# Two moves in VectorE's written order: batch 3's column maxima between the two halves of the fourth operand sum, batch 0's second softmax finished behind batch 2's own

## The chip, the cores and the metric

One NeuronCore of a Trainium2 chip runs the whole kernel. The metric is the device time of one execution in microseconds. Engine names below are those of the profile: PE is TensorE's matmuls and PEld its weight loads, DVE is VectorE, ACT is ScalarE, POOL is GpSimd, SP is the engine whose queue issues most of the DMAs.

## The reference

Cross-attention in both directions between 512 tokens and 32 state rows, for 8 batches of 8 heads, and behind it a feed-forward block on all rows.

```python
B, H, S, Ns, D = (8, 8, 512, 32, 64)
n_tokens, d_model, d_ff = (4608, 512, 2048)
...
scores = scale * np.matmul(x, state.transpose(0, 1, 3, 2))
scores = scores - scores.max(-1, keepdims=True)
a = np.exp(scores)
a /= a.sum(-1, keepdims=True) + 1e-09
xread = np.matmul(a, state)
scores2 = scale * np.matmul(state, x.transpose(0, 1, 3, 2))
scores2 = scores2 - scores2.max(-1, keepdims=True)
a2 = np.exp(scores2)
a2 /= a2.sum(-1, keepdims=True) + 1e-09
sread = np.matmul(a2, x)
return np.concatenate([xread, sread], axis=2).astype(np.float32)
...
h = x @ w_in
g = np.maximum(0.01 * h, h)
return (g @ w_out).astype(np.float32)
```

The second line of code gives the default sizes of the block; here it works on B x (512 + 32) = 4352 rows. The first softmax (of a token over the 32 state rows) feeds `xread`, the second (of a state row over the 512 tokens) feeds `sread`.

## The kernel before

**Tiling.** A batch's scores are one PSUM tile `sc` of 128 x 1024: the partitions hold 32 state rows for each of four heads, two such groups lie side by side, and the columns are the tokens. There is one `sc` bank pair for all batches, which also takes one of the products `pm` further on. The kernel does not form `xread`: it multiplies the state with `w_in` first (`a_m`, result `pm`, copied into SBUF as `M` by `m_evict` or by the copies at L1221 and L1229), and `ff1` multiplies `M` with the transposed probabilities `aT`. Each `ff1` makes 128 of the 2048 hidden rows for the batch's 512 tokens in a PSUM tile `ph`, two matmuls of 512 columns, and ACT's leaky ReLU (L398) writes it to `hT`. There are two `ph` buffers.

**The product with `w_out`** is done with seven half-size products instead of eight (`Fast` and `Batch`). They run in the order 1, 2, 6, 5, 7, 3, 4, and each has 8 units `(n, m)` of two matmuls (L674). Their left operands are parts of `hT` or sums of parts: four sums numbered 0 to 3, tiles `su0` to `su3`, computed on DVE by `sums` at L663. Each can be done in halves, `sums(n, 0, 4)` for units 0 to 3 and `sums(n, 4, 8)` for units 4 to 7. Product 6 takes sum 1, product 5 takes sum 0, product 7 takes sum 2, product 3 takes sum 3. Sum 1 is an input of sum 3. Product 4 takes a weight sum, the tile `tw_x` written at L640. Products 1, 6, 5 and 7 are saved by ACT (L683), the results are joined by DVE (L686) and by POOL (L746), and go out by DMA.

**First softmax of a batch.** `a_shift` finds each token's block maxima in `sc` (L221), spreads them (L229) and subtracts them (L234, result `sh`); `a_exp` is ACT's exponential (L241); `a_probs` sums, inverts and multiplies (L246 to L259, result `aT`).

**Second softmax.** `a_max2` takes the maxima along the rows of `sc`, one DVE reduce of 128 x 1024 (L283) and a small scaling of its 128 x 2 result (L285, `mcols`). `a_exp2` is two exponentials on ACT, one for each half of `sc` (L291); they need `mcols`, and they are the last readers of `sc`. `a_probs2` is what remains of that softmax: DVE adds 1e-9 to the 128 x 2 row sums (L297) and inverts them into the tile `qall` (L299). Nothing else is done there for batches 0 to 6: `a_sread_rows` multiplies the unnormalized `sread` (PSUM tile `psn`) with `qall` while it copies it out (L346).

**The order.** It is written out by hand: each engine runs its instructions in the order in which the program emits them, and waits only for semaphores. The loop over `b` runs batches 2 to 7, 16 steps `s` each. A step emits one `ff1` of batch `b` and some units of batch `b - 1`'s product with `w_out`. For `b == 2` the numbers of units are `PACE2 = (1, 2, 0, 4, 4, 4, 4, 4, 4, 4, 4, 4, 4, 5, 5, 5)`. Twelve of batch 1's 56 units are emitted ahead of the loop and four in steps 0 to 2, so steps 3 and 4 hold product 6, steps 5 and 6 product 5, steps 7 and 8 product 7, steps 9 and 10 product 3, and steps 11 and 12 product 4. Behind step 11's units PE runs the three `a_m` of batch 3, whose second writes into the `sc` banks and whose third takes both `ph` buffers.

DVE's part is emitted much earlier than PE needs it. In step 3 of `b == 2` the program emits, for DVE and in this order: `a_probs2(a0)`, the scaled copy in `a_sread_rows([a0])`, the first part of batch 3's `a_shift`, all of sum 2 of batch 1, the second part of `a_shift`, `a_max2` of batch 3, and the two halves of sum 3 of batch 1. Behind them, from step 7, come the second half of `tw_x` (L640), batch 3's `a_probs` and, from step 10, the join of product 3.

Four POOL copies `cast_x` of batch 4's tokens (L111) and POOL's copy of the later state rows (L181) are emitted in steps 3 and 4. SP's queue transposes batch 4's tokens by DMA behind that (L195, tile `xT`), for batch 4's scores in the next `b`.

Ahead of the loop, batch 2's `a_exp` and `a_probs` are emitted behind `piece(0, h0, 1, 3, copy=VEC)`, and what DVE gets next is the copy of batch 2's second `M` chunk (`m_evict(a2, 1, pm[0], VEC)`, L385).

Of the kernel before, what the change touches and what calls it, by code (L numbers as in the profile page):

```python
# [30 lines left out]
def kernel(  # L31
# [75 lines left out]
    def open_xb(b):  # L107
        xs[b] = xpool.tile([P, NT, H, D], BF16, name="xb", tag="xb")
# [80 lines left out]
    def a_open(a, b):  # L189
        a.b = b  # L190
        a.xb = xs[b]
        a.xT = att.tile([P, NT, NK, P], BF16, name="xT", tag="xT")
# [26 lines left out]
    def block_max(flat, n):  # L219
        m1 = att.tile([P, n], FP32, name="mrow", tag="mrow")  # L220
        nc.vector.tensor_reduce(  # L221
            out=m1[:], in_=flat.rearrange("p (c j) -> p c j", j=NS),
            axis=AX.X, op=ALU.max, apply_transpose=True,
        )
        return m1

    def block_rows(m1, n):
        m1b = att.tile([P, n, NS], FP32, name="mrowb", tag="mrowb", bufs=1)
        nc.vector.transpose(m1b[:], m1[:, :, None].to_broadcast([P, n, NS]))  # L229
        return m1b  # L230

    def block_sub(flat, m1b, n):
        sh = att.tile([P, n * NS], FP32, name="sh", tag="sh", bufs=1)
        nc.vector.tensor_tensor(  # L234
            out=sh[:], in0=flat, in1=m1b[:].rearrange("p c j -> p (c j)"), op=ALU.subtract,
        )
        return sh
# [26 lines left out]
    def a_shift(a, part=None):  # L264
        flat = a.sc[:].rearrange("p g c -> p (g c)")
        if part != 1:
            a.mb = block_rows(block_max(flat, NB), NB)
        if part != 0:
            a.sh = block_sub(flat, a.mb, NB)

    def a_exp(a):
        a.e1 = block_exp(a.sh, NB)

    def a_probs(a, part=None):
        if part != 1:
            a.q1h = block_recip(a.e1, NB)
        if part != 0:
            a.aT = att.tile([P, 2, S], BF16, name="aT", tag="aT")
            block_probs(a.aT[:], a.e1, a.q1h, NB)

    def a_max2(a):
        m2 = att.tile([P, 2], FP32, name="mcol", tag="mcol")
        nc.vector.tensor_reduce(out=m2[:], in_=a.sc[:], axis=AX.X, op=ALU.max, negate=True)  # L283
        a.m2s = att.tile([P, 2], FP32, name="mcols", tag="mcols")
        nc.vector.tensor_scalar(out=a.m2s[:], in0=m2[:], scalar1=SCALE, scalar2=None, op0=ALU.mult)  # L285
# [10 lines left out]
    def a_probs2(a):  # L296
        nc.vector.tensor_scalar(out=a.r2[:], in0=a.r2[:], scalar1=1e-9, scalar2=None, op0=ALU.add)  # L297
        q2 = qall[:, a.b]
        nc.vector.reciprocal(q2, a.r2[:])  # L299
        if a.b == B - 1:  # L300
            a.a2 = att.tile([P, 2, S], BF16, name="a2", tag="e2", bufs=3)
            for g in range(2):
                nc.vector.tensor_scalar(
                    out=a.a2[:, g, :], in0=a.e2[:, g, :],
                    scalar1=q2[:, g:g + 1], scalar2=None, op0=ALU.mult,
                )
# [456 lines left out]
    a0, a1, a2 = att_of[:3]  # L763
# [283 lines left out]
    before = Batch(1, h1)  # L1047
# [34 lines left out]
    piece(0, h0, 1, 3, copy=VEC)  # L1082
    a_exp(a2)
    a_probs(a2)
    a_open(att_of[3], 3)
    a_xt_dma(att_of[3])
    ff(10, 12, 13)
# [21 lines left out]
    for b in range(2, B):  # L1109
        hT = hpool.tile([P, 16, S], BF16, name="hT", tag="hT")  # L1110
        a = att_of[b]
        nxt = att_of[b + 1] if b + 1 < B else None
        now = Batch(b, hT)

        def fill(s):
            units((PACE2 if b == 2 else PACE)[s])

        def units(n):
            left = min(n, len(before.units))
            if left:  # L1120
                before.run(left)
            if n > left:
                now.run(n - left)

        ms = 11 if b == 2 else 10
        for s in range(16):
            fast = nxt is None and 4 <= s < 12
            if fast:
                n = 1 if s in (7, 11) else 2
                k = PACE[s]  # L1130
                for i in range(n):
                    fl.product()
                    units((i + 1) * k // n - i * k // n)
            elif s == ms + 1:
                fill(s)
            elif s == 0 and b == 2:
                units(1)
            if not fast:
                ff1(a, hT, 4 + s if nxt is None and s < 4 else s)
            if s == 0:  # L1140
                if b + 2 < B:
                    load_x(b + 2, nc.sync)
                a_a2t(a)
                for n in (0, 1):
                    before.f.sums(n, 4, 8)
            elif s == (3 if b == 2 else 1):
                if nxt is not None:
                    a_scores(nxt)
                m_evict(a, 3, a_m(a, 3, "big"), SCA)
                if b == 2:  # L1150
                    a_probs2(a0)
                    a_sread_rows([a0])
                elif b % 2:
                    a_sread_rows([att_of[b - 2], att_of[b - 1]])
                if b == 2:
                    a_shift(nxt, 0)
                    before.f.sums(2)
                    a_shift(nxt, 1)
                    a_max2(nxt)
                    before.f.sums(3, 0, 4)  # L1160
                    before.f.sums(3, 4, 8)
                elif nxt is not None:
                    a_shift(nxt)
                if b + 2 < B:
                    open_xb(b + 2)
                    for h in range(0, H, 2):
                        cast_x(b + 2, h, h + 2, POO)
                if b > 2:
                    before.f.sums(2, 4, 8)
            elif s == 3:  # L1170
                before.f.sums(3)
                if nxt is not None:
                    a_max2(nxt)
            elif s == 4:
                if b == 2:
                    state_t(1)
                elif b == 4:
                    sread_t(0, 3)
                elif b == 7:
                    sread_t(1, 4)  # L1180
            elif s == 8:
                if nxt is None:
                    a_sread(a)
            elif s == (13 if b == 2 else 12):
                for n in range(3):
                    now.f.sums(n, 0, 4)
            if nxt is None:
                if s == 1:
                    fl = FastLast(a, hT)
                    fl.sums()  # L1190
                elif s in (6, 10):
                    fi.w_sum({6: 1, 10: 3}[s])
                elif s == 13:
                    fl.flush()
                    fi.x_sums()
            elif b >= B - 3 and s == 14:
                if b == B - 3:
                    fi = FastIn(None)
                fi.w_sum(2 * (b - (B - 3)))
            if s == (9 if b == 2 else 7) and b + 2 < B:  # L1200
                a_open(att_of[b + 2], b + 2)
                a_xt_dma(att_of[b + 2])
            if nxt is not None:
                if b == 2 and s < ms:
                    if s in (8, 9):
                        a_exp2(nxt, s - 8)
                    elif s == 7:
                        a_exp(nxt)
                        weights_sum(3, 0, 4)
                        a_probs(nxt, 0)  # L1210
                elif s == 5:
                    a_exp(nxt)
                elif s in (7, 8):
                    a_exp2(nxt, s - 7)
                    if s == 7:
                        a_probs(nxt)
                elif s == ms + 1:
                    for some in ((a1, a2, nxt) if b == 2 else (nxt,)):
                        a_probs2(some)
                elif s in (ms + 2, ms + 3):  # L1220
                    SCA(nxt.M[:, s - ms - 2, DM:2 * DM], pm1[:, s - ms - 2, :])  # L1221
            if s != ms + 1 and not fast:
                fill(s)
            if s == ms and nxt is not None:
                pm0 = a_m(nxt, 0, "big")
                pm1 = a_m(nxt, 1, "sc")
                pm2 = a_m(nxt, 2, "ph")
                for g, copy in enumerate((VEC, SCA)):
                    copy(nxt.M[:, g, 2 * DM:3 * DM], pm2[g][:])  # L1229
                m_evict(nxt, 0, pm0, SCA)  # L1230
                if b == 2:
                    a_probs(nxt, 1)
        before = now
# [90 lines left out]
```

## Time and profile before

| | us |
|---|---|
| median of 3 runs | 203.46 (203.34 to 203.77) |
| the profiled execution's own time | 203.29 |
| its span, first to last instruction | 201.5 |
| PE busy | 194.9 (97%) |
| DVE busy | 160.4 (80%) |
| ACT busy | 144.1 (72%) |
| POOL busy | 54.3 (27%) |

All times in the rows further down are microseconds from the span's start. A row of the timeline gives start, duration, engine, line, operation, the tiles written and read with their shapes, the count of instructions merged into it, and in brackets how long the engine was idle before it and what ended that. Neighbouring matmuls overlap in their durations, so their distance is read from start to start. In the view of waits, the numbers are the total, the count and the longest.

### The profile page before, as it was taken

The numbers are of one execution on the slowest core, as the hardware profiler recorded it, in microseconds if no ns is written. First come the engines' busy times: TensorE is split into PE (matmuls) and PEld (weight loads), VectorE is DVE, ScalarE is ACT, GpSimd is POOL, SyncE is SP. The second block draws the span as 40 slices with busy tenths as digits, with TensorE's granted clock in tenths as the row PEclk, the third lists the DMA queues.
The fourth block names the chain that finished last, engine by engine and source line by source line (L and its number), as shares of the span: only waits on it lengthen the run. The fifth ranks groups of instructions, "written<-read, shape, count | busy, mean of one in ns | idle before, by whom it ended". The sixth has DMA issues, their size and how long they took to land.

```text
span 201.5 us, 4991 instructions
## 1 busy us (share of the span) xinstructions
PE 194.9 (97%) x2066; PEld 134.4 (67%) x2066; DVE 160.4 (80%) x246; ACT 144.1 (72%) x264; POOL 54.3 (27%) x79
## 2 busy tenths in 40 slices
PE   7799999999999999999999999999999999999992
PEld 2467644346676667766776677676767688799881
DVE  1666779998999989975997599779978977995622
ACT  3468837699877866978697868787878768767610
POOL 8751065591028004200420040200020024004250
PEclk9999999999999999999999999999999999999998
DMA  6999997999581894449433844290025102310035
GB/s 166 226 208 258 249 293 132 217 278 219 109 228 28 236 281 74 93 176 265 84 71 143 279 72 87 104 157 6 0 107 156 29 0 89 123 55 0 0 96 167
DMA packets 40470, 28.01 MB, mean 139 GB/s; under 512 B 25280, under 2 KB 37696, under 8 KB 40448
## 3 DMA queue, kind: packets, MB, share of 16 engines
q1 hardware_dynamic: 35248, 20.88, 41.3%
q0 software_dynamic: 4912, 6.55, 15.8%
q10 hardware_dynamic: 288, 0.26, 0.5%
q8 instruction: 16, 0.26, 0.5%
q14 instruction: 6, 0.05, 0.1%
HBM read 17.30 MB, written 8.91 MB: 130 GB/s over the span
## 4 chain that ended last, share of the span: by engine, by line
PE 74%; DMA 14%; DVE 6%; ACT 2%; POOL 1%; issue 1%; POOLq 0%; DVEq 0%
PE yq L674 40%; PE ph L392 19%; DMA xl<-in_x_dram 10%; DMA w_in_bf<-in_moe_w_in_dram 4%; PE pf L470 3%; PE yu L674 3%; PE pm L371 3%; DVE su L663 2%; PE pl L559 2%; PE psn L337 1%; PE py L603 1%; PE phw L405 1%; PE sc L211 1%; ACT e L291 1%; DVE mrowb L229 1%
## 5 line engine op out<-in xcount | busy, mean ns | idle before, releaser
L398 ACT ACTIVATE hT<-ph 128x512 bf16<-128x512 f32 x100 | 58.7, 604 | 18.5 <-PE ph L392 18.1
L392 PE MATMUL ph<-aT,M 128*128 128x512 bf16 x200 | 57.9, 379 | 0.0
L674 PEld LDWEIGHTS <-su 128*128 128x128 bf16 x480 | 45.8, 98 | 15.4 <-DVE su L663 1.9
L674 PEld LDWEIGHTS <-hT 128*128 128x128 bf16 x336 | 32.3, 98 | 14.3 <-issue 2.5
L674 PE MATMUL yq<-tw_xf,su 128*128 128x256 bf16 x224 | 31.6, 273 | 0.0
L674 PE MATMUL yq<-w_out_bf,hT 128*128 128x256 bf16 x224 | 31.0, 273 | 0.0
L111 POOL CAST xb<-xl 128x512 bf16<-128x512 f32 (+1 forms) x24 | 13.4, 604 | 48.8 <-DMA xl<-in_x_dram 37.6
L663 DVE TENSOR_TENSOR su<-hT 128x1024 bf16<-128x1024 bf16 (+1 forms) x27 | 19.3, 718 | 6.7 <-ACT hT L398 6.7
L392 PEld LDWEIGHTS <-M 128*128 128x128 bf16 x200 | 19.4, 98 | 5.7 <-issue 0.5
L746 POOL TENSOR_TENSOR yo<-sv,sv 128x512 f32<-128x512 f32 x7 | 9.5, 1358 | 41.2 <-issue 20.8
L683 ACT COPY sv<-yq 128x512 f32<-128x512 f32 x28 | 16.3, 586 | 3.0 <-PE yq L674 2.2
L674 PE MATMUL yq<-w_out_bf,su 128*128 128x256 bf16 x112 | 15.3, 273 | 0.4 <-DVE su L663 0.4
L674 PE MATMUL yq<-tw_x,su 128*128 128x256 bf16 x112 | 15.5, 273 | 0.0
L686 DVE TENSOR_TENSOR yo<-yq,sv 128x512 f32<-128x512 f32 x20 | 13.6, 682 | 1.5 <-PE yq L674 1.5
L674 PE MATMUL yq<-tw_x,hT 128*128 128x256 bf16 x104 | 14.5, 273 | 0.0
L385 ACT CAST M<-pm 128x1024 bf16<-128x1024 f32 x12 | 12.2, 1019 | 0.2 <-PE pm L371 0.2
L291 ACT ACTIVATE e<-sc,mcols 128x512 bf16<-128x512 f32 x16 | 11.0, 696 | 0.1
L603 PEld LDWEIGHTS <-hT 128*128 128x128 bf16 x64 | 5.9, 98 | 7.2 <-issue 1.1
L663 DVE TENSOR_TENSOR su<-su,hT 128x1024 bf16<-128x1024 bf16 x14 | 9.7, 692 | 0.5
L283 DVE TENSOR_REDUCE mcol<-sc 128x2 f32<-128x1024 f32 x8 | 9.7, 1216 | 0.0
L221 DVE TRANSPOSE_TENSOR_REDUCE mrow<-sc 128x32 f32<-128x1024 f32 x7 | 8.7, 1242 | 0.5 <-PE sc L211 0.5
L663 DVE TENSOR_TENSOR su<-hT,su 128x2048 bf16<-128x2048 bf16 (+1 forms) x8 | 9.0, 1134 | 0.0
(173 smaller groups left out, 301.7 us busy)
## 6 DMA issues: line engine op xcount, KB each, us to landing
out_dram<-yo SPq DMA_DIRECT2D x12, 512.0 KB, 2.7
xl<-in_x_dram SPq DMA_DIRECT2D x5, 1024.0 KB, 6.8
w_in_bf<-in_moe_w_in_dram POOLq DMA_DIRECT2D x4, 512.0 KB, 9.6
w_out_bf<-in_moe_w_out_dram POOLq DMA_DIRECT2D x4, 512.0 KB, 17.4
xf<-in_x_dram SPq DMA_DIRECT2D x2, 512.0 KB, 5.5
x<-in_x_dram POOLq DMA_DIRECT2D x2, 512.0 KB, 13.9
xl<-in_x_dram POOLq DMA_DIRECT2D x1, 1024.0 KB, 20.1
out_dram<-ysb SPq DMA_DIRECT2D x4, 256.0 KB, 5.6
```

The lines of the kernel that those rows point to most:

```text
L111: copy(xs[b][:, :, h0:h1].rearrange("p t h d -> p h t d"), xl[b][:, h0:h1].rearrange("p h (t d) -> p h t d", t=NT),)
L221: nc.vector.tensor_reduce(out=m1[:], in_=flat.rearrange("p (c j) -> p c j", j=NS), axis=AX.X, op=ALU.max, apply_transpose=True,)
L283: nc.vector.tensor_reduce(out=m2[:], in_=a.sc[:], axis=AX.X, op=ALU.max, negate=True)
L291: nc.scalar.activation(out=a.e2[:, g], in_=a.sc[:, g, :], func=AF.Exp, bias=a.m2s[:, g:g + 1], scale=SCALE, accum_out=a.r2[:, g:g + 1],)
L385: copy(a.M[:, :, cols], pm[:])
L392: nc.tensor.matmul(ph[:], lhsT=a.M[:, g, P * j:P * (j + 1)], rhs=a.aT[:, g, :], start=(g == 0), stop=(g == 1),)
L398: nc.scalar.activation(out=hT[:, j, :], in_=ph[:], func=AF.Prelu, alpha=0.01)
L663: (eng or nc.vector).tensor_tensor(out=S[n][:, ms], in0=u[:, ms], in1=v[:, ms], op=op)
L674: nc.tensor.matmul(bank[:, i, :], lhsT=lhs[:, m, P * i:P * (i + 1)], rhs=rhs[:, m, :], start=(first and m == 0 and (i == 0 or of is not No ...
L683: copy(t[:], bank)
L686: nc.vector.tensor_tensor(out=dst, in0=bank, in1=self.sv[n][:], op=ALU.add)
L746: nc.gpsimd.tensor_tensor(out=self.yo(1)[:, :, HC:], in0=f.sv[7][:], in1=f.sv[5][:], op=ALU.add)
```

## The change

Two edits, both in DVE's order alone. No instruction is added or removed, and no other engine's order changes.

1. `a_probs2(a0)` (L297 and L299, batch 0) leaves its place ahead of `a_sread_rows([a0])` in step 3 of `b == 2` and goes ahead of the loop, right behind batch 2's `a_probs`.
2. In the same step, `sums(3, 0, 4)` of batch 1 is emitted ahead of `a_max2` of batch 3 instead of behind it. `sums(3, 4, 8)` stays behind.

```diff
@@ -1082,6 +1082,7 @@
     piece(0, h0, 1, 3, copy=VEC)
     a_exp(a2)
     a_probs(a2)
+    a_probs2(a0)
     a_open(att_of[3], 3)
     a_xt_dma(att_of[3])
     ff(10, 12, 13)
@@ -1148,7 +1149,6 @@
                     a_scores(nxt)
                 m_evict(a, 3, a_m(a, 3, "big"), SCA)
                 if b == 2:
-                    a_probs2(a0)
                     a_sread_rows([a0])
                 elif b % 2:
                     a_sread_rows([att_of[b - 2], att_of[b - 1]])
@@ -1156,8 +1156,8 @@
                     a_shift(nxt, 0)
                     before.f.sums(2)
                     a_shift(nxt, 1)
+                    before.f.sums(3, 0, 4)
                     a_max2(nxt)
-                    before.f.sums(3, 0, 4)
                     before.f.sums(3, 4, 8)
                 elif nxt is not None:
                     a_shift(nxt)
```

## The prediction

> **What bounds the kernel now.** I read the page's busy shares first, then PE's waits behind the place of the change, then the timelines of PE and DVE there.
>
> ```profile
> PE 194.9 (97%) x2066; PEld 134.4 (67%) x2066; DVE 160.4 (80%) x246; ACT 144.1 (72%) x264; POOL 54.3 (27%) x79
> ```
>
> ```profile
> PE yq L674 <- DVE su L663: 0.4, 1, 0.4
> ```
>
> PE is busy for 97% of the span. The second fence is the whole answer on PE's waits from 61 us to the end: one wait, of a unit's matmul for an operand sum of DVE. Behind it PE sets its own pace, so what is taken from this wait should come off the end. PE's timeline around it:
>
> ```profile
> 52.90 0.42 PE L337 MATMUL psn<-xb,a2T 128*32 128x64 bf16 x32
> ...
> 59.36 0.59 PE L392 MATMUL ph<-aT,M 128*128 128x512 bf16 x2
> 59.79 1.04 PE L674 MATMUL yq<-tw_x,su 128*128 128x256 bf16 x8
> 60.66 0.59 PE L392 MATMUL ph<-aT,M 128*128 128x512 bf16 x2
> 61.63 1.05 PE L674 MATMUL yq<-w_out_bf,su 128*128 128x256 bf16 x8 [0.37 <-DVE su L663]
> 62.51 0.59 PE L392 MATMUL ph<-aT,M 128*128 128x512 bf16 x2
> 62.95 1.04 PE L674 MATMUL yq<-w_out_bf,su 128*128 128x256 bf16 x8
> 63.82 0.59 PE L392 MATMUL ph<-aT,M 128*128 128x512 bf16 x2
> 64.25 1.04 PE L674 MATMUL yq<-tw_x,hT 128*128 128x256 bf16 x8
> 65.22 0.84 PE L371 MATMUL pm<-w_in_bf,st_t 64*32 64x512 bf16 x24
> ```
>
> A step's two `ff1` matmuls take 0.43 from start to start (59.36 to 59.79), and its eight of the product 0.87 (59.79 to 60.66). Product 3 should begin at 60.66 + 0.43 = 61.09. It begins at 61.63, so the stall costs 0.54; the bracket's 0.37 counts from the modelled end of the matmul in front. Its releaser is the first half of sum 3. DVE's own order shows why it is late:
>
> ```profile
> 48.43 0.69 DVE L259 TENSOR_TENSOR aT<-e,qb 128x1024 bf16<-128x1024 bf16 x1
> 49.56 1.23 DVE L385 CAST M<-pm 128x1024 bf16<-128x1024 f32 x1 [0.44 <-PE pm L371]
> ...
> 53.35 0.68 DVE L686 TENSOR_TENSOR yo<-yq,sv 128x512 f32<-128x512 f32 x1
> 53.96 0.16 DVE L297 TENSOR_SCALAR r<-r 128x2 f32<-128x2 f32 x1
> 54.15 0.17 DVE L299 RECIPROCAL qall<-r 128x2 f32<-128x2 f32 x1
> 54.42 0.29 DVE L346 TENSOR_TENSOR sr_n<-psn,qall 128x128 bf16<-128x128 f32 x1
> ...
> 58.17 1.22 DVE L234 TENSOR_TENSOR sh<-sc,mrowb 128x1024 f32<-128x1024 f32 x1
> 59.31 1.21 DVE L283 TENSOR_REDUCE mcol<-sc 128x2 f32<-128x1024 f32 x1
> 60.55 0.43 DVE L285 TENSOR_SCALAR mcols<-mcol 128x2 f32<-128x2 f32 x1
> 60.90 0.68 DVE L663 TENSOR_TENSOR su<-hT,su 128x1024 bf16<-128x1024 bf16 x1
> 61.50 1.09 DVE L663 TENSOR_TENSOR su<-hT,su 128x1024 bf16<-128x1024 bf16 x1
> 62.51 1.09 DVE L640 TENSOR_TENSOR tw_x<-tw_xf,w_out_bf 128x1024 bf16<-128x1024 bf16 x1
> 65.28 0.63 DVE L686 TENSOR_TENSOR yo<-yq,sv 128x512 f32<-128x512 f32 x1
> 66.12 0.69 DVE L1229 CAST M<-pm 128x512 bf16<-128x512 f32 x1 [0.21 <-PE pm L371]
> ```
>
> DVE has no idle time from 49.56 to 65.91 (65.28 + 0.63), then waits 0.21 for PE. It is a backlog. The column maxima (59.31 to 60.90 with the scaling) stand ahead of both halves of sum 3; the first half ends at 60.90 + 0.68 = 61.58 and PE starts 0.05 later.
>
> **Edit 1, `a_probs2(a0)` earlier.** At its old place the pair takes 53.96 to 54.42, 0.46 until the next instruction starts. That next one, L346, also needs PE's `psn`, which ended at 52.90 + 0.42 = 53.32, so it can start at 53.96 and everything behind it 0.46 earlier. At the new place DVE idles from 49.12 to 49.56 for PE. At the old place the pair's start overlapped the end of its predecessor by 0.07 (54.03 against 53.96), so the pair takes 49.05 to 49.51 and is hidden by that wait. Cost at the new place: 0. Without that cover it would push L385 and all behind it by up to 0.46 and merely give the edit's gain back. Its inputs are row sums that ACT left before the loop, and no DMA moves with it. I take 0 cost; the ends are 0 and 0.46.
>
> **Edit 2, first half of sum 3 ahead of the maxima.** L234 starts at 58.17 - 0.46 = 57.71 and its successor at 59.31 - 0.46 = 58.85. That successor is now the half sum, done at 59.53, against a need at 61.09. The stall of 0.54 goes. Late next could be the second half. The maxima start 0.60 behind the half sum (60.90 to 61.50), at 59.45; the scaling 1.24 later, at 60.69; the second half 0.35 behind that, at 61.04. It takes between 0.68 and 1.09 and ends between 61.72 and 62.13. PE wants it at 62.95 - 0.54 = 62.41, less the 0.05 of release. So no new stall: 0.23 are left in the worse of these rows.
>
> The two durations of one instruction need an explanation, and it is POOL:
>
> ```profile
> 59.23 2.82 POOL L111 CAST xb<-xl 128x512 bf16<-128x512 f32 x4 [13.37 <-DMA xl<-in_x_dram]
> 62.00 1.07 POOL L181 CAST stb<-stf 128x512 bf16<-128x512 f32 x1
> 63.03 1.70 POOL L746 TENSOR_TENSOR yo<-sv,sv 128x512 f32<-128x512 f32 x1
> ...
> 76.74 2.29 POOL L111 CAST xb<-xl 128x512 bf16<-128x512 f32 x4 [12.01 <-DMA xl<-in_x_dram]
> ```
>
> Four copies take 2.29 with little of such work beside them, 0.57 each, and 2.82 here; and here the sums, the weight sum and the scaling on DVE are slow as well. They hinder each other. The bound for the second half: the scaling and the half sum each wait out a whole copy of 0.57. Then the scaling clears at 60.69 + 0.57 + 0.08 = 61.34, the sum ends at 61.34 + 0.57 + 0.68 = 62.59, and PE is late by 62.64 - 62.41 = 0.23. The price of this step is 0 to 0.23. I take 0, as the measured sum of this very stretch (1.09) is the nearest row.
>
> The Trainium skill has a rule for this, in "SBUF — State Buffer", section "Who interferes with whom": a Vector instruction with two SBUF inputs contends with a GpSimd instruction that reads SBUF, and whichever comes second waits until the other has finished. The rows above agree: 1.09 - 0.68 = 0.41 is less than one copy of 0.57. By that rule the total would be a gain of 0.54 if the second half comes first and of 0.31 if it comes second twice; by the rows alone 0.54. The rows decide for 0.54.
>
> **What the later maxima delay.** ACT's second exponential waits for them.
>
> ```profile
> 61.02 0.69 ACT L291 ACTIVATE e<-sc,mcols 128x512 bf16<-128x512 f32 x1
> ...
> 62.17 0.61 ACT L398 ACTIVATE hT<-ph 128x512 bf16<-128x512 f32 x1
> 62.66 0.70 ACT L291 ACTIVATE e<-sc,mcols 128x512 bf16<-128x512 f32 x1
> ...
> 64.45 0.60 ACT L398 ACTIVATE hT<-ph 128x512 bf16<-128x512 f32 x1 [0.52 <-PE ph L392]
> ```
>
> The scaling ends at 60.69 + 0.43 = 61.12 instead of 60.98, so these exponentials start 0.14 later, and with them the ReLUs behind them in ACT's order. The ReLU at 62.17 ends at 62.17 + 0.14 + 0.61 = 62.92 and frees the buffer of the `ff1` that PE wants at 63.82 - 0.54 = 63.28. The second exponential releases `sc` at 62.66 + 0.14 + 0.70 = 63.50, and the `a_m` wants it at 65.22 - 0.54 = 64.68. The ReLU at 64.45 had an idle 0.52 ahead of it, so ACT absorbs a shift of 0.14 there while PE comes 0.54 earlier (0.52 - 0.54 - 0.14: about 0.16 late), ending near 64.67, before the third `a_m` needs the buffer. Cost: 0.
>
> **DVE's next tight place.** L1229 empties a `ph` buffer for the next `ff1`. DVE is free at 65.91 - 0.46 = 65.45, and PE's result is there at 66.12 - 0.54 = 65.58. PE still ends last, by 0.13. Cost 0; past that margin every 0.1 of DVE costs PE 0.1.
>
> **SP's queue and the DMAs.** Nothing passes them, but batch 4's transposed tokens come by DMA and PE will ask 0.54 earlier.
>
> ```profile
> 64.37 1.80 SPq L195 DMA_TRANSPOSE xT<-xb  x1
> ...
> DMA to landing us min/median/max: 4.3/4.3/4.3
> ```
>
> ```profile
> 73.12 0.34 PE sc L211 x8
> ```
>
> Issued at 64.37 they land at 68.67, almost four microseconds ahead of the scores that PE then starts at 72.58. Cost 0.
>
> **The sum.** Edit 1 costs 0 and removes 0.46 of DVE work in front of the tight places; edit 2 removes 0.54 of PE stall; new waits 0. The profiled execution took 203.29 (a span of 201.5 and 1.79 around it): 203.29 - 0.54 = 202.75. The median of the runs lies 0.17 above that execution, so I forecast 203.46 - 0.54 = 202.92, in short 202.9. A measurement of this kernel tells about 0.2%, or 0.41 us, from no change; this gain is 0.27%, just past it.
>
> **Rivals.**
> 1. The second half of sum 3 takes over the wait: PE stalls 0.23 in step 10, and the gain is 0.31, 203.15. For it: every DVE instruction there that met a copy was slowed. Against it: it needs two full waits. A stronger form, in which edit 1 gives nothing because the wait at 49.56 gets shorter, moves the second half 0.46 later, to 62.18 to 62.59, which ends in about the same time.
> 2. The change doesn't do what it says: PE comes 0.54 early to another wait and loses it there. The place would be L1229: DVE without its 0.46 would be free at 65.91 and let PE have only 0.21 of the 0.54, 203.25; with a slip of another 0.2 nothing is left, 203.46. For it: DVE's margin there is 0.13. Against it: the pair has an idle gap of 0.44 to go into.
> 3. Slower: POOL wins at every meeting. The scaling and the half sum wait out a copy each (0.57 twice) and the weight sum at L640 waits out POOL's add, 1.27 by another execution of it; the scaling's time elsewhere stands beside it:
>
> ```profile
> 81.87 0.17 DVE L285 TENSOR_SCALAR mcols<-mcol 128x2 f32<-128x2 f32 x1
> 83.94 1.27 POOL L746 TENSOR_TENSOR yo<-sv,sv 128x512 f32<-128x512 f32 x1 [4.92 <-issue]
> ```
>
>    That is 2.41 of waiting in place of the 0.26 (the scaling's 0.43 against 0.17), 0.41 (second half) and 0.41 (L640) of now, 1.33 more. DVE reaches L1229 at 65.45 + 1.33 = 66.78, 0.66 later than now: 204.1. It decides from the point where the extra waiting is over 65.45 to 66.12, 0.67. Against it: POOL's add comes behind a fifth copy, so L640 would hardly meet it at its start. The rule of the Trainium skill quoted above ("SBUF — State Buffer", "Who interferes with whom") would allow this with the worst order of issue; in the trace DVE and POOL took turns.
>
> **How the numbers follow.** The whole stall goes: 0.66, with 202.7 to 203.15 as its own range (the runs lie from 0.12 below to 0.31 above their median). Rival 1: 0.14. Rival 2: 0.12. Rival 3: 0.08. The range runs from 202.65 to 203.5: the upper end takes in rivals 1 and 2 and leaves rival 3 out, and a tenth at most lies beyond the lower. Faster by over 0.2% means below 203.05: nine tenths of the forecast's case and a little of rival 1, 0.61. Slower means above 203.87: rival 3 and a remainder of rival 2, 0.10. The rest, 0.29, is within.
>
> **What would show it.** In the profile of the changed kernel: L297 and L299 once near 49.1 with L385 unmoved at 49.56; L346 near 53.96; the first half of sum 3 near 58.85 and the maxima behind it; the first matmuls of product 3 at 61.09 without a bracket, and PE without any wait for `su` behind 61; L1229 near 65.58, still released by PE. Wrong would be: a wait of PE for `su` at 62.4, a bracket at the `ff1` behind L1229 (now 66.87), or scores of batch 4 still at 73.12 and not at 72.58.

## The result

The changed kernel takes 202.86 us (median of 22 runs, 202.43 to 203.72), the kernel before 203.48 in the same series (22 runs, 203.04 to 205.4). The ratio is 0.9966 with a 95% interval of 0.9952 to 0.998: 0.4 to 1.0 us less. 202.9 was forecast, with a gain of 0.54; the medians differ by 0.62.

The profiled execution does not show this in its span: 201.6 us, against 201.5 before. PE's waits do: from 50 us to the end the changed kernel's view of them has no line at all. (An empty view is not proof by itself: with edit 2 alone, further down, it is empty too and PE still loses 0.17. The distances from start to start decide.) Its PE timeline:

```profile
53.72 1.05 PE L674 MATMUL yq<-tw_xf,su 128*128 128x256 bf16 x8
...
61.13 0.59 PE L392 MATMUL ph<-aT,M 128*128 128x512 bf16 x2
61.56 1.04 PE L674 MATMUL yq<-w_out_bf,su 128*128 128x256 bf16 x8
...
63.74 0.59 PE L392 MATMUL ph<-aT,M 128*128 128x512 bf16 x2
64.17 1.04 PE L674 MATMUL yq<-tw_x,hT 128*128 128x256 bf16 x8
65.14 0.84 PE L371 MATMUL pm<-w_in_bf,st_t 64*32 64x512 bf16 x24
```

Product 3 starts 61.56 - 61.13 = 0.43 behind its `ff1`, with no bracket: the stall is gone. But product 6 starts at 53.72, and in the kernel before it started at 53.25:

```profile
53.25 1.05 PE L674 MATMUL yq<-tw_xf,su 128*128 128x256 bf16 x8
```

That shift of 0.47 is older than the first edit. ACT's copy of batch 2's tokens, which waits for their DMA, already differs. First before, then changed:

```profile
32.65 1.05 ACT L111 CAST xb<-xl 128x1024 bf16<-128x1024 f32 x1 [0.79 <-DMA xl<-in_x_dram]
```

```profile
33.00 1.04 ACT L111 CAST xb<-xl 128x1024 bf16<-128x1024 f32 x1 [0.66 <-DMA xl<-in_x_dram]
```

The program up to there is the same, so 0.35 of the shift is the landing of a transfer in that one execution. Over all profiles here product 6 starts anywhere from 52.91 to 53.72. In ten of the thirteen it follows this copy by 20.60 to 20.75; in the other three by 21.06 to 21.37, and what held PE there stays open. So I read the experiments in two stretches of PE: from the start of product 6 to batch 3's three `a_m` (L371), which holds everything that the change touches, and from there to the last group of matmuls. Before, the first is 65.22 - 53.25 = 11.97; now it is 65.14 - 53.72 = 11.42, which is 0.55 less. The second was 131.58 before and is 131.78 in this execution; in its two later profiles the changed kernel had 131.58 and 131.59, so that 0.20 is no property of the change.

DVE's timeline of the changed kernel shows the two edits at their new places:

```profile
49.12 0.69 DVE L259 TENSOR_TENSOR aT<-e,qb 128x1024 bf16<-128x1024 bf16 x1
49.73 0.16 DVE L297 TENSOR_SCALAR r<-r 128x2 f32<-128x2 f32 x1
49.93 0.17 DVE L299 RECIPROCAL qall<-r 128x2 f32<-128x2 f32 x1
50.03 1.23 DVE L385 CAST M<-pm 128x1024 bf16<-128x1024 f32 x1
...
54.42 0.28 DVE L346 TENSOR_TENSOR sr_n<-psn,qall 128x128 bf16<-128x128 f32 x1
...
59.30 0.68 DVE L663 TENSOR_TENSOR su<-hT,su 128x1024 bf16<-128x1024 bf16 x1
59.89 1.22 DVE L283 TENSOR_REDUCE mcol<-sc 128x2 f32<-128x1024 f32 x1
61.14 0.45 DVE L285 TENSOR_SCALAR mcols<-mcol 128x2 f32<-128x2 f32 x1
61.50 0.68 DVE L663 TENSOR_TENSOR su<-hT,su 128x1024 bf16<-128x1024 bf16 x1
62.10 1.09 DVE L640 TENSOR_TENSOR tw_x<-tw_xf,w_out_bf 128x1024 bf16<-128x1024 bf16 x1
...
64.38 0.55 DVE L250 TENSOR_SCALAR r<-r 128x32 f32<-128x32 f32 x1
...
66.05 0.69 DVE L1229 CAST M<-pm 128x512 bf16<-128x512 f32 x1 [0.18 <-PE pm L371]
```

Counted from the start of product 6, L385 stands at 50.03 - 53.72 = -3.69, where it stood before (49.56 - 53.25 = -3.69). That alone would not show a delay of both, so here is PE ahead of the pair, first before, then changed:

```profile
42.91 1.03 PE L603 MATMUL py<-w_out_bf,hT 128*128 128x512 bf16 x4
```

```profile
43.38 1.03 PE L603 MATMUL py<-w_out_bf,hT 128*128 128x512 bf16 x4
```

From there to product 6 PE takes 10.34 in both, so the pair costs nothing at its new place. L346 moves from 1.17 to 0.70, 0.47 earlier. The first half of sum 3 ends at 59.98, 1.58 ahead of PE, and the second at 62.18, 0.69 ahead of PE's 62.87.

### The profile page after: what moved, and what is told of

It is laid out like the page before. It is cut to its first block, busy times and chain, and to the rows that moved or that the text cites. A ratio compares the mean times of both kernels' runs of the same rounds, so it can differ in the third digit from the quotient of the medians.

```text
span 201.6 us, 4990 instructions
## 1 busy us (share of the span) xinstructions
PE 195.2 (97%) x2066; PEld 134.8 (67%) x2066; DVE 161.5 (80%) x246; ACT 143.9 (71%) x264; POOL 54.6 (27%) x79
## 4 chain that ended last, share of the span: by engine, by line
PE 80%; DMA 14%; ACT 2%; POOL 1%; issue 0%; DVE 0%; POOLq 0%
PE yq L674 43%; PE ph L392 22%; DMA xl<-in_x_dram 10%; DMA w_in_bf<-in_moe_w_in_dram 4%; PE pf L470 3%; PE pm L371 3%; PE yu L674 3%; PE pl L559 2%; PE psn L337 1%; PE sc L211 1%; PE py L603 1%; PE phw L405 1%; ACT e L291 1%; ACT xb L111 1%; ACT M L383 0%; PE yz L674 0%
## 5 line engine op out<-in xcount | busy, mean ns | idle before, releaser
L111 POOL CAST xb<-xl 128x512 bf16<-128x512 f32 (+1 forms) x24 | 14.6, 653 | 50.8 <-DMA xl<-in_x_dram 50.8
L385 ACT CAST M<-pm 128x1024 bf16<-128x1024 f32 x12 | 12.2, 1018 | 0.2 <-PE pm L371 0.2
L663 DVE TENSOR_TENSOR su<-hT,su 128x2048 bf16<-128x2048 bf16 (+1 forms) x8 | 9.5, 1183 | 0.0
```

The source lines that it names most:

```text
L111: copy(xs[b][:, :, h0:h1].rearrange("p t h d -> p h t d"), xl[b][:, h0:h1].rearrange("p h (t d) -> p h t d", t=NT),)
L385: copy(a.M[:, :, cols], pm[:])
L663: (eng or nc.vector).tensor_tensor(out=S[n][:, ms], in0=u[:, ms], in1=v[:, ms], op=op)
```

## The experiments

All are read by the two stretches and by their own runs against the kernel before on the same chip. The kernel before has one profile, so its 11.97 is that of one execution.

| kernel | product 6 starts | product 6 to `a_m` | `a_m` to last matmuls | median, before beside it | ratio, 95% |
|---|---|---|---|---|---|
| before | 53.25 | 11.97 | 131.58 | | |
| changed | 53.72 | 11.42 | 131.78 | 202.86, 203.48 | 0.9966 (0.9952 to 0.998) |
| edit 1 alone | 53.04 | 11.42 | 131.58 | 202.62, 203.09 | 0.9979 (0.997 to 0.9988) |
| edit 2 alone | 53.01 | 11.58 | 131.59 | 202.65, 203.09 | 0.9979 (0.997 to 0.9988) |
| sum 3 whole ahead of the maxima | 53.31 | 12.11 | 131.59 | 203.06, 203.09 | 0.9996 (0.9986 to 1.0007) |
| before, POOL's copies late | 53.27 | 11.86 | 131.59 | 202.98, 203.09 | 0.9995 (0.9986 to 1.0005) |
| changed, again | 53.16 | 11.42 | 131.58 | 202.52, 203.19 | 0.9972 (0.9962 to 0.9981) |
| edit 1 alone, again | 52.91 | 11.42 | 131.89 | 202.65, 203.19 | 0.9981 (0.9972 to 0.9991) |
| changed, one reduce more | 53.22 | 11.42 | 132.76 | 203.55, 203.19 | 1.0027 (1.0015 to 1.0039) |
| changed, POOL's copies late | 52.98 | 11.41 | 131.59 | 202.48, 203.19 | 0.9971 (0.9962 to 0.9979) |
| changed, third time | 53.44 | 11.41 | 131.59 | 202.93, 203.42 | 0.9975 (0.9963 to 0.9987) |
| edit 1 alone, third time | 53.53 | 11.42 | 131.59 | 203.0, 203.42 | 0.997 (0.9946 to 0.9994) |
| edit 2 alone, POOL's copies late | 53.56 | 11.42 | 131.59 | 202.96, 203.42 | 0.9968 (0.9946 to 0.999) |

### Edit 1 alone

```diff
     a_probs(a2)
+    a_probs2(a0)
     a_open(att_of[3], 3)
...
                 if b == 2:
-                    a_probs2(a0)
                     a_sread_rows([a0])
```

> The kernel before with edit 1 alone: batch 0's pair (L297, L299) behind batch 2's a_probs, the column maxima still ahead of both halves of sum 3. My theory (DVE's backlog hands its lateness to PE one for one, and each edit takes its own piece of it): L346 starts 0.46 earlier relative to PE, the first half of sum 3 ends 0.46 earlier, and PE's stall at the start of product 3 shrinks from 0.54 to about 0.08. Total about 203.48 - 0.46 = 203.0. Rival A (the reordering of edit 2 alone carries the gain, the pair is hidden either way): PE's wait for su stays near 0.4 to 0.5 and the time stays at 203.5.

The stall does not shrink to 0.08, it is gone, and the whole 0.55 with it: 0.47 by the medians, 11.42 by the stretch. Edit 1's DVE and PE rows:

```profile
59.86 0.20 DVE L285 TENSOR_SCALAR mcols<-mcol 128x2 f32<-128x2 f32 x1
59.97 1.69 DVE L663 TENSOR_TENSOR su<-hT,su 128x1024 bf16<-128x1024 bf16 x2
```

```profile
53.04 1.05 PE L674 MATMUL yq<-tw_xf,su 128*128 128x256 bf16 x8
...
60.88 1.04 PE L674 MATMUL yq<-w_out_bf,su 128*128 128x256 bf16 x8
...
64.46 0.84 PE L371 MATMUL pm<-w_in_bf,st_t 64*32 64x512 bf16 x24
```

The half sum starts 59.97 - 53.04 = 6.93 behind product 6, against 7.65 before: 0.72 earlier, not 0.46. The pair accounts for 0.47. The rest is that the scaling L285 took 0.20 here and 0.43 before. It was that fast in all three profiles of edit 1 alone; why POOL's copies held it up so little there is not shown. Rival A falls.

### Edit 2 alone

```diff
                     a_shift(nxt, 1)
+                    before.f.sums(3, 0, 4)
                     a_max2(nxt)
-                    before.f.sums(3, 0, 4)
                     before.f.sums(3, 4, 8)
```

> The kernel before with edit 2 alone: the first half of sum 3 ahead of the maxima, the pair still in front of L346. My theory: the stall at product 3 goes (0.54), but DVE is still 0.46 later than in the changed kernel, so the second half of sum 3 ends between 62.2 and 62.6 against a need at 62.36 (a new wait of 0 to 0.23), and L1229 starts at 65.91 at the earliest, released by DVE's own order and not by PE, which leaves 0.21 of the gain: about 203.27, and a bracket at an ff1 behind L1229 of about 0.3. Rival A (edit 2 alone carries it): the whole 0.54, 202.9, with L1229 still waiting for PE.

More is left than I expected: 0.39 by the stretch and 0.44 by the medians, against my 0.21. And PE loses the remainder at another place. Its PE and ACT timelines:

```profile
62.16 1.04 PE L674 MATMUL yq<-w_out_bf,su 128*128 128x256 bf16 x8
63.20 0.59 PE L392 MATMUL ph<-aT,M 128*128 128x512 bf16 x2
```

```profile
61.40 0.69 ACT L291 ACTIVATE e<-sc,mcols 128x512 bf16<-128x512 f32 x1 [0.67 <-DVE mcols L285]
61.98 0.19 ACT L291 ACTIVATION_READ_ACCUMULATOR e<-sc,mcols 128x1 f32 x1
62.07 0.58 ACT L683 COPY sv<-yq 128x512 f32<-128x512 f32 x1
62.54 0.61 ACT L398 ACTIVATE hT<-ph 128x512 bf16<-128x512 f32 x1
```

The `ff1` of step 11 starts at 63.20 where 62.16 + 0.87 = 63.03 was due. The ReLU that frees its `ph` buffer ends at 62.54 + 0.61 = 63.15. ACT waited 0.67 for the scaled maxima ahead of it. So the later maxima cost PE 0.17 by way of exponential, ReLU and buffer; L1229 was no limit.

### Sum 3 whole ahead of the maxima

```diff
                     before.f.sums(3, 0, 4)
-                    a_max2(nxt)
                     before.f.sums(3, 4, 8)
+                    a_max2(nxt)
```

> The changed kernel with both halves of sum 3 ahead of the maxima instead of one. My theory: PE needs neither half sooner than the changed kernel gives it, so nothing is gained on PE; the maxima and with them ACT's two exponentials come about 0.6 later than in the changed kernel, which ACT's 0.5 of idle time and the margin of more than 1 us on the sc banks absorb nearly: the same time as the changed kernel, 202.9, at most 0.2 more. Rival B (the exponentials are close to the next limit, and splitting the sum around the maxima is what makes the change work): PE waits at the a_m or at the ff1 behind the ReLUs by 0.3 or more, 203.2 or above.

My theory fell and rival B held, more strongly than it said: nothing is left of the gain. PE's timeline and ACT's:

```profile
62.45 1.04 PE L674 MATMUL yq<-w_out_bf,su 128*128 128x256 bf16 x8
64.03 0.59 PE L392 MATMUL ph<-aT,M 128*128 128x512 bf16 x2 [0.54 <-ACT hT L398]
```

```profile
62.23 0.69 ACT L291 ACTIVATE e<-sc,mcols 128x512 bf16<-128x512 f32 x1 [1.40 <-DVE mcols L285]
```

The `ff1` of step 11 is 64.03 - (62.45 + 0.87) = 0.71 late, more than the stall that was removed. The bracket names the ReLU. The first exponential comes 62.23 - 53.31 = 8.92 behind product 6, in the changed kernel 61.62 - 53.72 = 7.90:

```profile
61.62 0.69 ACT L291 ACTIVATE e<-sc,mcols 128x512 bf16<-128x512 f32 x1 [0.38 <-DVE mcols L285]
...
62.77 0.61 ACT L398 ACTIVATE hT<-ph 128x512 bf16<-128x512 f32 x1
```

There the ReLU ends at 63.38 and the `ff1` wants the buffer at 63.74: a margin of 0.36. It gives a rule for both experiments: 1.02 later, less 0.36, is 0.66 against the 0.71 lost; for edit 2 alone, with 61.40 - 53.01 = 8.39, it is 8.39 - 7.90 - 0.36 = 0.13 against 0.17. In both the `ff1` starts 0.05 behind the end of its ReLU, which makes up the difference. The maxima have to go between the halves, not behind them.

### POOL's copies of batch 4's tokens in step 9

In the kernel before, `cast_x(4, ...)` is emitted behind POOL's add of product 7 instead of ahead of it.

```diff
-                    for h in range(0, H, 2):
+                    for h in range(0, H, 2) if b > 2 else ():
                         cast_x(b + 2, h, h + 2, POO)
...
             if s == (9 if b == 2 else 7) and b + 2 < B:
+                for h in range(0, H, 2) if b == 2 else ():
+                    cast_x(b + 2, h, h + 2, POO)
                 a_open(att_of[b + 2], b + 2)
```

> The kernel before with POOL's four copies of batch 4's tokens emitted in step 9 instead of step 3, behind POOL's add of product 7 (L746), so that they no longer run beside DVE's backlog at 59 to 62. My theory (POOL and DVE hold each other up on SBUF): L285 takes 0.17 instead of 0.43 and all halves of sum 3 take 0.68, the first half of sum 3 ends about 0.27 earlier and PE's stall falls from 0.54 to about 0.27: about 203.2, if batch 4's transposed tokens still land ahead of their scores at 73.1. Rival C (the long durations have nothing to do with POOL): L285 and the second half stay at 0.43 and 1.09, the stall stays, 203.5.

The durations came out as expected, the stall did not. DVE's timeline, then POOL's, then PE's wait:

```profile
53.97 0.32 DVE L297 TENSOR_SCALAR r<-r 128x2 f32<-128x2 f32 x1
...
60.72 0.17 DVE L285 TENSOR_SCALAR mcols<-mcol 128x2 f32<-128x2 f32 x1
60.80 1.29 DVE L663 TENSOR_TENSOR su<-hT,su 128x1024 bf16<-128x1024 bf16 x2
62.00 0.68 DVE L640 TENSOR_TENSOR tw_x<-tw_xf,w_out_bf 128x1024 bf16<-128x1024 bf16 x1
```

```profile
53.65 0.61 POOL L181 CAST stb<-stf 128x512 bf16<-128x512 f32 x1 [7.54 <-DMA stf<-in_state_dram]
```

```profile
61.54 1.05 PE L674 MATMUL yq<-w_out_bf,su 128*128 128x256 bf16 x8 [0.49 <-DVE su L663]
```

Without the copies L285 takes 0.17, both halves together 1.29, the weight sum 0.68: rival C falls, the slow rows are POOL's doing. But POOL's copy of the state rows, which had stood behind those copies, now ran at 53.65 and met DVE's L297, which took 0.32 instead of 0.16. So the half sum started only 7.65 - 7.53 = 0.12 earlier, the stall fell by 0.10, and the time did not move clearly. (The bracket grew to 0.49 only because the record of the second `ff1` matmul in front is missing from this trace; from start to start the stall is 61.54 - 60.67 - 0.43 = 0.44.) The Trainium skill ("SBUF — State Buffer", "Who interferes with whom") counts `tensor_scalar` among the VectorE instructions that can contend with GpSimd, and says that the second waits until the first has finished. L285 and L297 are of this kind, and the trace agrees: the copy ended at 53.65 + 0.61 = 54.26 and L297 at 54.29.

### The changed kernel with one more reduce on DVE

```diff
                         a_probs(nxt, 0)
+                        dose = consts.tile([P, 2], FP32, name="dose")
+                        nc.vector.tensor_reduce(
+                            out=dose[:], in_=w_out_bf[:, 0:2, :], axis=AX.X, op=ALU.max,
+                        )
```

> The changed kernel with one more reduce on DVE (128 x 1024 bf16 of w_out into a scratch tile that nothing reads, 1.22 by the rows of such reduces) behind batch 3's a_probs sums and ahead of the join of product 3. My theory (past its margin, DVE's lateness at L1229 goes to PE one for one): the margin there is 0.18, so PE waits 1.22 - 0.18 = 1.04 at the ff1 behind L1229, and the time is 1.0 above the changed kernel, 203.9. Rival E (PE has other work queued that hides a late L1229, or ph's other buffer bridges it): 0.6 or less, down to nothing.

203.55 against 202.52 for the changed kernel on the same chip: 1.03 for a forecast of 1.04. The size is right, the place only in part.

```profile
66.29 0.59 PE L392 MATMUL ph<-aT,M 128*128 128x512 bf16 x2
67.55 0.59 PE L392 MATMUL ph<-aT,M 128*128 128x512 bf16 x2 [0.66 <-DVE M L1233]
67.98 1.25 PE L674 MATMUL yq<-w_out_bf,hT 128*128 128x256 bf16 x10
69.07 0.59 PE L392 MATMUL ph<-aT,M 128*128 128x512 bf16 x2
69.50 1.56 PE L674 MATMUL yq<-w_out_bf,hT 128*128 128x256 bf16 x10
```

(The copy of L1229 is at L1233 in this file.) The first `ff1` behind it did not wait at all. The second came at 67.55 instead of 66.29 + 0.43, 0.83 late, and a group of ten further on took 1.56 instead of 1.25: 0.31 more. So L1229 itself has 0.43 more room than I gave it, and a second consumer, further down, has less. Rival E falls: together they make 1.14 of the 1.18 by which the second stretch is longer.

This profile holds more lateness than the reduce brought. An addition on DVE ahead of the reduce, L250, took 1.11 here and 0.55 in the changed kernel:

```profile
63.73 1.11 DVE L250 TENSOR_SCALAR r<-r 128x32 f32<-128x32 f32 x1
```

With it and the reduce, which took 1.07 from start to start, the join of product 3 came 13.00 behind product 6 instead of 11.52, which is 1.48 later, and L1229 came 13.59 - 12.33 = 1.26 later. Less the 0.43 of room that is the 0.83 which PE lost, so past the real margin the lateness goes to PE one for one. That the medians met the forecast of 1.04 is in part luck: its margin, 0.18, was too small by the 0.43, and the loss at the second consumer was not in it. The profiled execution took 203.9, 0.35 more than the median; what the others lost, and where, is not recorded.

### Edit 1 alone, again, beside the changed kernel

> The changed kernel again, beside edit 1 alone on the same chip. By the first four profiles the stretch of PE from the start of product 6 to batch 3's a_m is 11.97 before, 11.42 in the changed kernel and 11.42 with edit 1 alone. My theory (edit 1 alone already ends the stall, edit 2 adds only margin): 11.42 again and the same time as edit 1 alone, about 0.55 below the kernel before. Rival D (edit 2 adds what the first run of edit 1 showed by luck of POOL's copies): faster than edit 1 alone by about 0.1 to 0.2.

> Edit 1 alone, again. My theory: a stretch of 11.42 to 11.5 with no wait of PE for su above 0.1, and about 0.55 below the kernel before. Rival D: where the scaling L285 meets one of POOL's copies and takes 0.43 as in the kernel before, the first half of sum 3 ends 0.25 later than in the first run of edit 1, some 0.07 behind PE's need, and the stretch is 11.5.

The changed kernel repeats its 11.42. Edit 1 alone has 11.42 too, but lost 0.31 behind `a_m`. Its DVE rows and the weight load that waited:

```profile
63.73 1.11 DVE L250 TENSOR_SCALAR r<-r 128x32 f32<-128x32 f32 x1
...
65.69 0.68 DVE L1229 CAST M<-pm 128x512 bf16<-128x512 f32 x1
...
68.16 0.68 DVE L686 TENSOR_TENSOR yo<-yq,sv 128x512 f32<-128x512 f32 x1
```

```profile
68.90 0.75 PEld L674 LDWEIGHTS <-hT 128*128 128x128 bf16 x7 [0.32 <-issue]
```

L250, an addition to 32 numbers per partition, took 1.11 beside POOL's add:

```profile
63.54 1.27 POOL L746 TENSOR_TENSOR yo<-sv,sv 128x512 f32<-128x512 f32 x1
```

It ended at 64.84, 0.03 behind the add. In the changed kernel's first profile it started further into the add, took 0.55 and ended 0.04 behind it. In the kernel before it had nothing of POOL beside it:

```profile
64.79 0.18 DVE L250 TENSOR_SCALAR r<-r 128x32 f32<-128x32 f32 x1
```

The 1.11 pushed the join of product 4 to 68.16; it ended at 68.84, and PE's next product started its load at 68.90. The join empties a bank that this product takes over. The profile does not name the releaser, only its time fits, and it fits twice: with one reduce more the join ended at 69.97 and the load started at 70.03. In the changed kernel's second profile the join ended 0.44 earlier against product 6 (15.49 behind it instead of 15.93), with no wait.

### Whether edit 2 adds time, and the copies once more

> The changed kernel a third time, again beside edit 1 alone, to see whether edit 2 adds time and not only margin. So far the changed kernel was 0.62 and 0.67 below the kernel before and edit 1 alone 0.47 and 0.54, with intervals that overlap. If edit 2 adds something: 0.1 to 0.2 below edit 1 alone once more. If it adds only margin: within 0.1 of it. The stretch of PE from product 6 to a_m should be 11.42 again.

> Edit 1 alone a third time. In its second profile the stretch from product 6 to a_m was 11.42, but DVE's small instruction L250 waited 0.9 beside POOL's add, L1229 came 0.46 after PE's result, and PE lost 0.31 behind the join of product 4. If that is a matter of when POOL's copies arrive, this profile shows 0 or 0.3 there; L250 near 0.55 with nothing lost, or near 1.1 with a loss.

This time edit 1 alone lost nothing: L250 at 0.55, second stretch 131.59. Over the three series edit 1 alone is 0.47, 0.54 and 0.42 below the kernel before, both edits 0.62, 0.67 and 0.49; the intervals of the ratios overlap where both ran side by side. In the third series the ratios even stand the other way round (0.9975 with both, 0.997 with edit 1). Whether edit 2 adds about 0.1 stays open.

Rival D was not put to the test either. Its condition, L285 held up by a copy, did not occur with edit 1 alone: L285 took 0.20, 0.19 and 0.18 in the three profiles, against 0.45, 0.47 and 0.45 in the changed kernel's. By the first profile the half sum ended at 59.97 + 0.68 = 60.65, and PE wanted it at 60.88 - 0.05 = 60.83. The 0.23 by which L285 was slower in the kernel before would use up these 0.18 and make PE wait 0.05, so edit 2 would be worth about that much in such an execution. This is an estimate; no run shows it.

> The changed kernel with POOL's four copies of batch 4's tokens in step 9 as in the earlier run. My theory (with the stall gone, DVE's time beside the copies costs nothing any more): DVE gains about 0.5 to 0.8 in front of L1229, seen as a longer wait of L1229 for PE, the stretch from product 6 to a_m stays 11.42, and the time is that of the changed kernel. Rival F (DVE's slowing by POOL still costs PE): the stretch falls below 11.4 and the time by 0.2 or more.

With both edits and POOL's copies late DVE has plenty of time, and it is worth nothing:

```profile
65.30 0.69 DVE L1231 CAST M<-pm 128x512 bf16<-128x512 f32 x1 [1.11 <-PE pm L371]
```

L1229 (L1231 in that file) now waits 1.11 for PE instead of 0.18. The stretch is 11.41 and the time 202.48 against 202.52. Rival F falls.

> Edit 2 alone, with POOL's four copies in step 9. With edit 2 alone PE lost 0.17 at the ff1 of step 11, for which I hold ACT's later exponentials responsible (scaling, exponential, ReLU, ph buffer). My theory: without the copies the scaling L285 takes 0.17 instead of 0.44, the exponentials come about 0.15 to 0.25 earlier, the loss at that ff1 falls to 0.05 or less and the stretch from 11.58 to 11.42 to 11.47; about 0.5 below the kernel before. Rival G (the 0.17 has another cause, such as DVE's tw_x or the pair itself): the stretch stays at 11.55 or more.

Edit 2 alone without the copies beside it: the stretch falls from 11.58 to 64.98 - 53.56 = 11.42.

```profile
61.46 0.17 DVE L285 TENSOR_SCALAR mcols<-mcol 128x2 f32<-128x2 f32 x1
```

```profile
61.66 0.69 ACT L291 ACTIVATE e<-sc,mcols 128x512 bf16<-128x512 f32 x1 [0.40 <-DVE mcols L285]
```

The exponential comes 8.10 behind product 6 instead of 8.39, which is inside 7.90 + 0.36, and the `ff1` is on time. Rival G falls.

## Why the prediction was right, point by point

- **What bounds the kernel.** Right. The one wait of PE behind 61 us was worth its 0.54: the stretch fell by 0.55, no later wait took it back, and the median fell by 0.62.
- **Edit 1, cost 0 at its new place.** Right: L385 did not move against PE. But the cover was thinner than the 0.44 that the profile before showed: the pair filled all of it and L385 follows without a bracket, because DVE ran 0.22 later against PE there in that execution. It still fitted because it is shorter at its new place than I priced it: 0.30 from start to start (49.73 to 50.03) and not 0.46. At the old place L346, which reads `qall`, starts 0.27 behind L299; here L385, which does not, starts 0.10 behind it. At 0.46 the pair would have pushed L385 by 0.16, so the cost of 0 was partly luck.
- **Edit 2 removes the stall.** The effect was right, the sharing was not. I gave the 0.54 to edit 2 and to edit 1 only a margin. Edit 1 alone removes the stall in three profiles, in all of them with a quick L285. Edit 2 alone removes it too, but pays 0.17 back at the `ff1` of step 11, which leaves 0.39. The gains don't add: each takes DVE's lateness at the same place.
- **The second half of sum 3.** I had it end 0.23 ahead of PE in the worse of the quoted rows; it ended 0.69 ahead, since it took 0.68 and POOL hindered the weight sum behind it instead. Rival 1 didn't come. The step's idea, that DVE and POOL hinder each other, was confirmed by taking the copies away.
- **What the later maxima delay.** The margin of 0.36 at the `ff1` of step 11 (63.28 less 62.92) was the measured one, 63.74 less 63.38. I passed over it as "cost 0". It is the nearest limit of this change: half a sum more in front of the maxima uses it up and loses the whole gain.
- **DVE's next tight place.** The margin was right in size (0.13 forecast; 0.18, 0.14 and 0.18 of idle time in the three profiles) but put at the wrong consumer. L1229 frees the buffer of the second `ff1` behind it, 0.43 later than I took; what has little room is the join of product 4 in DVE's order behind it. That DVE's lateness past the margin goes to PE one for one held at that `ff1`: 1.26 later, less 0.43, cost 0.83. Rival 2 needed this margin to be used up; in the changed kernel it was not.
- **Rival 3.** Not seen. The meeting that I priced highest, DVE with POOL's add, does occur, at L250 and not at L640, and cost 0.31 in one profile of edit 1 alone, and 0.31 again with one reduce more.
- **The DMA, the sum and the median.** The scores of batch 4 were on time. That the profiled execution differs from the median was allowed for, but not that the two profiled executions would differ by 0.47 in the part that is the same; a comparison of the two spans would have shown a loss of 0.1.

## What to carry to other kernels

When an in-order engine's backlog makes the bounding engine wait, pieces of work moved into an earlier idle gap, or behind the late result, remove the same wait, each up to its own length, so price them as alternatives and not as a sum. Then follow what the postponed work feeds: here the maxima had 0.36 us to spare by way of exponential, ReLU and a buffer, and one half sum more in front of them gave back all that was won. Compare profiles between two marks on the bounding engine, not by their spans, when the gain is no larger than what the start-up varies.

## What was not expected of the hardware

An addition to 128 x 32 numbers on VectorE (L250), 0.18 us alone, took 0.53 to 0.55 in seven of the thirteen profiles and 1.11 in two, where it met a GpSimd add of 1.26 or 1.27 near its start; in proportion to its own length that is the longest wait in the rows quoted here. And one and the same kernel (edit 1 alone) brought PE to the same instruction anywhere from 52.91 to 53.53 us, which is as much as the change is worth.
